# Where the second normalisation of the next token block is issued in the MLP loop of a state-space and MLP layer

## The chip, the cores and the metric

The kernel runs on one core of one Trainium2 chip. The metric is the device time of one execution in microseconds (us). The matrix multiplies run on TensorE (PE in the profile; its weight loads are listed as PEld), the rest on VectorE (DVE), ScalarE (ACT) and GpSimd (POOL). SyncE (SP) starts most of the transfers. Each engine works through its own list of instructions in the order in which the program put them there.

## What is computed

The layer has two halves on 2048 tokens of 640 channels. The first normalises the tokens, runs a short and a long convolution over them and adds the gated result to the input. The second normalises again and applies an MLP with a squared relu. Cut to what matters:

```python
def _layernorm(x, axis=-1, eps=1e-5):
    m = jnp.mean(x, axis=axis, keepdims=True)
    v = jnp.var(x, axis=axis, keepdims=True)
    return (x - m) / jnp.sqrt(v + eps)

def _B_ref(x, w1, b1, w2, b2):          # w1: 640 x 1728, w2: 1728 x 640
    h = jnp.einsum("bsd,df->bsf", x, w1) + b1
    r = jnp.where(h > 0, h, 0)
    h = r * r
    return jnp.einsum("bsf,fd->bsd", h, w2) + b2

h = _layernorm(x) * (1 + ca) + sa
x = x + ga * _A_ref(h, k, v, shift_k, ssm_k, ssm_D)
h = _layernorm(x) * (1 + cb) + sb
x = x + gb * _B_ref(h, w1, b1, w2, b2)
```

The vectors sa, ca, ga, sb, cb and gb come from one small conditioning vector. The change lies in the last two lines, in the second normalisation.

## The kernel before, in words

The first 290 us or so are the convolution half, and the change doesn't touch them. The MLP half goes through the tokens in `NC` = 8 blocks of 256 (n = 0 to 7), and in each block through the 1728 hidden channels in `NF` = 14 groups (f = 0 to 13; thirteen of 128 and a last one of 64). The loop at the end of the kernel (from line 1206) has one step for each pair (n, f), and the work of one pair is spread over several steps. A step i puts these pieces down, in this order:

- `mlp_back` of the pair three steps earlier (`MLAG` = 3): the second matrix multiply, twelve matmuls at L790, which reads the hidden values from a ring of buffers (`hring`) and adds into four accumulators in PSUM.
- `mlp_split` of the pair one step earlier: ScalarE copies the squared values to a high half (L146, in the helper `copy`), VectorE subtracts to get the low half (L157, in the helper `sub`). Both halves go to `hring`.
- `mlp_front` of this pair: the first matrix multiply, fifteen matmuls at L720 (ten at L711 for the last group), into one of two PSUM buffers.
- `mlp_front_end` of this pair: relu with bias on ScalarE (L752), then the square on GpSimd (L151).
- what prepares the next block, n + 1, spread over the steps of block n.

The preparation of block n + 1 goes like this for n of 1 and more. At f = 3 the block's 256 tokens are loaded (`load_x1`). At f = 5 VectorE makes means and variances, and at f = 6 ScalarE takes the root and VectorE makes the two vectors `rs2` and `nm2`. `prep_hat(n + 1, i)` (L670) then normalises 128 tokens by 640 channels in one ScalarE instruction at L672, i = 0 for the first 128 tokens of the block and i = 1 for the second. The result goes to `ML["xh"][i]`, which is a part of the tile `mtmp`; the relu's output lies in other parts of that tile. From f = 8 to f = 12 `prep_xt(n + 1, b)` handles one of five groups of 128 channels in each step: two transposes on TensorE (L685), one from each `ML["xh"][i]`, a scale and shift on VectorE (L687), a copy to the high half on ScalarE and a subtraction to the low half on GpSimd. While n is 0 the same work for block 1 has other places, since the weights are still being loaded then.

After the block's last group `mlp_end` and `mlp_out` use the same two `ML["xh"]` buffers for the gated output; this ends in the step f = 2 of the next block.

All instructions of an engine are tied into the order in which they were put down (`keep_order`, L118), so the place of a call in the loop decides what stands ahead of it and behind it on its engine. The two calls before the change, from L1236:

```python
                if f - (5 if n == 0 else 7) in (0, 1):
                    prep_hat(n + 1, f - (5 if n == 0 else 7))
                if f >= 8 and f - 8 < NB:
                    (prep_xt if n else prep_xt2)(n + 1, f - 8)
```

Of the kernel before, what the change touches and what calls it, by code (L numbers as in the profile page):

```python
# [92 lines left out]
def ssm_mlp_kernel(  # L93
# [549 lines left out]
    def stats2(n):  # L643
        for l in (2 * n, 2 * n + 1):
            if n:
                dve_stats(mv2[:, l], X1t[n][:, l - 2 * n])
            else:
                dve.bn_aggr(mv2[:, l], st2[:, l])

    def stats2_root(n):  # L650
        s = slice(2 * n, 2 * n + 2)
        act.activation(rs2[:, s], mv2[:, s, 1], AF.Sqrt, bias=eps_t)

    def stats2_end(n):
        s = slice(2 * n, 2 * n + 2)
        dve.reciprocal(rs2[:, s], rs2[:, s])
        dve.scalar_tensor_tensor(
            nm2[:, s], mv2[:, s, 0], -1.0, rs2[:, s], op0=ALU.mult, op1=ALU.mult
        )

    def load_x1(n):
        if n >= 2:
            X1t[n] = x1_tile(n)
            sp_dma(
                X1t[n], x1_d[n * CH : (n + 1) * CH, :].rearrange("(l p) d -> p l d", p=P)
            )
# [3 lines left out]
    def prep_hat(n, i):  # L670
        l = 2 * n + i
        act.activation(  # L672
            ML["xh"][i], X1t[n][:, i], AF.Identity, scale=rs2[:, l : l + 1], bias=nm2[:, l : l + 1]
        )
# [5 lines left out]
    def prep_xt1(n, b):  # L680
        if b == 0:
            XT[n] = sb.tile([P, 2, NB, CH], F32R, tag=f"XP{(n + 1) % 2}", name=f"xt_{n}")
        t = ps.tile([P, 2, P], F32, tag="Y", name=f"xtp_{n}_{b}", bufs=2)
        for i in range(2):
            pe.transpose(t[:, i], ML["xh"][i][:, b * P : (b + 1) * P], ident)  # L685
        f = ML["xf"][b % 2]
        dve.tensor_scalar(  # L687
            f,
            t.rearrange("p i s -> p (i s)"),
            cbs[:, 1, b : b + 1],  # L690
            cbs[:, 0, b : b + 1],
            op0=ALU.mult,
            op1=ALU.add,
        )
# [10 lines left out]
    def mlp_front(n, f, b):  # L705
        m = P if f < NF - 1 else 64
        if b == 0:
            hps[n, f] = ps.tile([P, CH], F32, tag="T", name=f"h_{n}_{f}", bufs=2)
        if m < P:
            for x in range(2):  # L710
                pe.matmul(  # L711
                    hps[n, f],
                    WI[1, f][:, b],
                    XT[n][:, x, b],
                    start=(b == 0 and x == 0),
                    stop=(b == NB - 1 and x == 1),
                )
            return
        for i, (a, x) in enumerate(((0, 0), (0, 1), (1, 0))):
            pe.matmul(  # L720
                hps[n, f][:m],
                WI[1, f][:, a, b],
                XT[n][:, x, b],
                start=(b == 0 and i == 0),
                stop=(b == NB - 1 and i == 2),
            )
# [15 lines left out]
    def mlp_front_end(n, f):  # L742
        m = P if f < NF - 1 else 64
        r = ML["r"][(n * NF + f) % 3]
        h = hps.pop((n, f))
        if m < P:

            act.activation(r[:m], h[m:], AF.Identity, bias=b1t[:m, f : f + 1])
            add(dve, r[:m], h[:m], r[:m])
            act.activation(r[:m], r[:m], AF.Relu)  # L750
        else:
            act.activation(r[:m], h[:m], AF.Relu, bias=b1t[:m, f : f + 1])  # L752
        mul(pool, r[:m], r[:m], r[:m])


    def mlp_split(n, f):
        m = P if f < NF - 1 else 64
        k = n * NF + f
        r = ML["r"][k % 3]
        if k == 2:  # L760
            hr = sb.tile([P, 4, 2, CH], F32R, tag="UP0", name="hring")
            ML["h"] += [hr[:, i] for i in range(4)]
        h = ML["h"][k % 6]
        if m == P:
            copy(act, h[:, 0], r)
            sub(dve, h[:, 1], r, h[:, 0])
        else:
            copy(act, h[:m, 0], r[:m])
            sub(dve, h[m:, 0], r[:m], h[:m, 0])
        hs[n, f] = h  # L770

    def mlp_back(n, f):
        if f == 0:
            accs[n] = [
                ps.tile([P, 320], F32, tag="X", name=f"acc_{n}_{i}", bufs=4) for i in range(4)
            ]
        acc = accs[n]
        h, w = hs[n, f], WI[2, f]
        if f < NF - 1:
            terms = ((0, 0), (0, 1), (1, 0))  # L780
        else:
            terms = ((0, 0), (0, 1))
        order = [(s, ti, i) for s in range(2) for ti in range(len(terms)) for i in range(2)]
        if f == NF - 1:
            order.sort(key=lambda o: (o[0], o[2]))
        for s, ti, i in order:
            if True:
                a, y = terms[ti]
                if True:
                    pe.matmul(  # L790
                        acc[2 * s + i],
                        h[:, a, s * P : (s + 1) * P],
                        w[:, y, i * 320 : (i + 1) * 320],
                        start=(f == 0 and ti == 0),
                        stop=(f == NF - 1 and ti == len(terms) - 1),
                    )

    def mlp_end(n):
        for s in range(1 if n == NC - 1 else 2):
            mlp_gate(n, s, 0)  # L800
            mlp_gate(n, s, 1)
# [5 lines left out]
    def mlp_out(n):  # L807
        for s in range(2):
            t = ML["xh"][s]
            l = 2 * n + s  # L810
            if n < NC - 1:
                add(dve if s else pool, X1t[n][:, s], t, X1t[n][:, s])
                sp_dma(out[l * P : (l + 1) * P, :], X1t[n][:, s])
                continue
            for i in range(2):
                o = slice(i * 320, (i + 1) * 320)
                if s:
                    mlp_gate(n, s, i)
                add(dve if s else pool, X1t[n][:, s, o], t[:, o], X1t[n][:, s, o])
                (act.dma_start if i else sp_dma)(out[l * P : (l + 1) * P, o], X1t[n][:, s, o])  # L820
# [363 lines left out]
    def residual(n, i, eng):  # L1184
        add(eng, X1t[n][:, i], X1t[n][:, i], row1b[0])

    def beside(f):
        n = min(len(stage), 6 + 2 * f)
        if f == 2:
            stats2(1)  # L1190
        while wn[0] < n:
            w_high()
        while wn[1] < n:
            w_low(dve)
        while len(stage) - wn[1] < 4 and items:
            load_item()
        if f < 3:
            finish_add(NB - 1, f + 1)
        if f == 0:
            finish_near(NB - 1, 1)  # L1200
        if f == 2:
            stats2_root(1)
        if f == 3:
            stats2_end(1)
# [3 lines left out]
    for i in range(len(seq) + MLAG):  # L1208
        if i >= MLAG:
            n, f = seq[i - MLAG]  # L1210
            mlp_back(n, f)
            if f == NF - 1:
                mlp_end(n)
        if 0 < i <= last + 1:
            mlp_split(*seq[i - 1])
        if i >= MLAG and f == NF - 1:
            mlp_out(n)
        if i <= last:
            n, f = seq[i]
            if i >= 2:  # L1220
                for b in range(NB):
                    mlp_front(n, f, b)
            mlp_front_end(n, f)
            if n == 0:
                if f >= 8 and f - 8 < NB:
                    prep_xt1(n + 1, f - 8)
                beside(f)
            if n + 1 < NC:
                if f == 3:
                    load_x1(n + 1)  # L1230
                if n and f == 5:
                    stats2(n + 1)
                if n and f == 6:
                    stats2_root(n + 1)
                    stats2_end(n + 1)
                if f - (5 if n == 0 else 7) in (0, 1):  # L1236
                    prep_hat(n + 1, f - (5 if n == 0 else 7))
                if f >= 8 and f - 8 < NB:
                    (prep_xt if n else prep_xt2)(n + 1, f - 8)
            if f >= 11 and f < 13:  # L1240
                residual(n, f - 11, pool)
# [25 lines left out]
```

## Time and profile before

| | us |
|---|---|
| median of 3 runs | 703.28 |
| lowest and highest run | 702.06, 704.84 |
| the profiled execution, its time | 705.5 |
| its span, first to last instruction | 703.7 |
| L720 matmuls, 1290 | 167.5 busy |
| L790 matmuls, 960 | 156.6 busy |
| L672 normalisations, 14 | 0.912 each (median) |
| mean clock granted to TensorE | 0.992 of full speed |

Times in the profile count from the first instruction of the profiled execution. A group in the profile is named by line, engine and operation, then what it writes and reads ("mtmp<-x,nm,rs" writes mtmp from x, nm and rs). "Idle before" is the time in which the engine stood still just ahead of an instruction, with the one that released it. The chain of work is followed back from the last instruction, at each step to what released it or to the instruction before it on its engine. Matmuls are pipelined and overlap in the records, so the starts of the pieces of the chain tell more than their lengths, and the end of a matmul is modelled.

### The profile page before, as it was taken

What the parts mean: (1) busy time and instruction counts of PE and PEld (TensorE: products, weight loads), DVE (VectorE), ACT (ScalarE), POOL (GpSimd) and SP (SyncE); (2) the same over time, 40 slices, a digit from 0 to 9 for tenths busy, and PEclk for the clock granted to TensorE, in tenths of its full rate; (3) what the DMA queues carried; (4) which work ended last, traced back from release to release, by engine and by line L of the source; (5) the groups of instructions that cost most, each with busy time, mean ns of one, the idle gap of its engine ahead of it and who ended that gap; (6) DMA issues with size and microseconds to landing.
All of it is one profiled execution on the core that took longest, in us unless ns stands there. A gap on an engine that the chain in (4) does not pass through costs nothing.

```text
span 703.7 us, 21084 instructions
## 1 busy us (share of the span) xinstructions
PE 662.0 (94%) x9164; PEld 634.2 (90%) x9164; DVE 334.6 (48%) x601; ACT 329.6 (47%) x688; POOL 311.2 (44%) x390
## 2 busy tenths in 40 slices
PE   6699799999999989999999999999999999999997
PEld 5688788888898888899999999999999999999996
DVE  5257666657684886587522323323332322422313
ACT  4436556877967966566233333233233233233221
POOL 1053155459869859433514414315215215224213
PEclk9999999999999999999999999999999999999999
DMA  9887889798672645274010100200200200200001
GB/s 232 248 240 235 238 238 250 232 231 219 181 186 82 158 126 172 69 227 142 39 38 1 42 35 1 74 3 1 75 1 1 76 1 1 76 1 1 38 1 38
DMA packets 110960, 74.76 MB, mean 106 GB/s; under 512 B 48658, under 2 KB 96146, under 8 KB 110868
## 3 DMA queue, kind: packets, MB, share of 16 engines
q1 hardware_dynamic: 108912, 72.87, 36.5%
q8 instruction: 72, 1.18, 0.7%
q10 hardware_dynamic: 1892, 0.54, 0.3%
q14 instruction: 20, 0.16, 0.1%
q0 software_dynamic: 64, 0.01, 0.0%
HBM read 58.98 MB, written 14.42 MB: 104 GB/s over the span
## 4 chain that ended last, share of the span: by engine, by line
PE 83%; ACT 6%; DVE 5%; issue 3%; DMA 2%; POOL 1%; SPq 0%; DVEq 0%; ACTq 0%; POOLq 0%
PE acc L790 27%; PE h L720 25%; PE pa L383 5%; PE x L398 5%; PE qp L464 5%; PE y L541 5%; PE h L398 3%; PE t L530 2%; PE h L711 1%; PE xtp L685 1%; PE kt L239 1%; DVE wx L151 1%; ACT a L146 1%; PE vt L276 1%; PE gr L928 1%
## 5 line engine op out<-in xcount | busy, mean ns | idle before, releaser
L151 POOL TENSOR_TENSOR mtmp<-mtmp 128x256 f32<-128x256 f32 x112 | 71.4, 638 | 244.4 <-ACT mtmp L752 236.5
L720 PE MATMUL h<-xt,w_S 128*128 128x256 f32 x1290 | 167.5, 281 | 1.1 <-DVE w_S L157 1.1
L720 PEld LDWEIGHTS h<-xt,w_S 128*128 128x128 f32 x1290 | 161.7, 190 | 1.3 <-DVE w_S L157 1.3
L790 PE MATMUL acc<-w_S,hring 128*128 128x320 f32 x960 | 156.6, 311 | 0.2 <-DVE hring L157 0.2
L157 DVE TENSOR_TENSOR hring<-mtmp,hring 128x256 fp32r<-128x256 f32 x112 | 66.4, 593 | 162.6 <-ACT hring L146 162.6
L790 PEld LDWEIGHTS acc<-w_S,hring 128*128 128x128 f32 x960 | 142.0, 188 | 0.7 <-DVE hring L157 0.7
L752 ACT ACTIVATE mtmp<-h,b1t 128x256 f32<-128x256 f32 x104 | 49.4, 475 | 180.1 <-PE h L720 177.0
L146 ACT ACTIVATE hring<-mtmp 128x256 fp32r<-128x256 f32 x112 | 46.6, 416 | 48.5 <-POOL mtmp L151 47.5
L383 PE MATMUL pa<-wx,p 64*64 64x64 f32 x2560 | 49.7, 228 | 10.9 <-issue 5.3
L383 PEld LDWEIGHTS pa<-wx,p 64*64 64x64 f32 x2560 | 44.1, 141 | 17.2 <-issue 11.3
L146 ACT ACTIVATE a<-pa 128x512 f32<-128x512 f32 x80 | 43.6, 611 | 22.9 <-PE pa L383 22.8
L151 DVE TENSOR_TENSOR wx<-x,wx 128x512 f32<-128x512 f32 x64 | 41.0, 684 | 19.4 <-PE x L398 8.9
L541 PE MATMUL y<-wx,wx 128*64 128x64 f32 x1280 | 45.4, 226 | 4.5 <-ACT wx L146 2.7
L541 PEld LDWEIGHTS y<-wx,wx 128*64 128x64 f32 x1280 | 40.7, 139 | 9.5 <-issue 4.2
L687 DVE TENSOR_SCALAR we<-xtp,cbs 128x256 f32<-128x256 f32 x35 | 19.0, 544 | 61.1 <-PE xtp L685 61.1
L398 PE MATMUL x<-a,gb 128*64 128x128 f32 x640 | 43.8, 281 | 3.0 <-DVE wx L151 1.8
L398 PEld LDWEIGHTS x<-a,gb 128*64 128x64 f32 x640 | 37.7, 141 | 4.4 <-PE h L398 2.4
L261 DVE SCALAR_TENSOR_TENSOR KV<-kt,tap,KV 128x511 f32<-128x511 f32 (+2 forms) x48 | 35.9, 747 | 8.1 <-ACT ktail L146 6.3
L154 POOL TENSOR_TENSOR wm<-wm,wm 128x640 f32<-128x640 f32 x20 | 32.9, 1647 | 10.3 <-ACT wm L341 10.0
L146 ACT ACTIVATE q<-qp 128x512 f32<-128x512 f32 (+1 forms) x40 | 21.3, 585 | 33.1 <-PE qp L464 33.1
L157 POOL TENSOR_TENSOR we<-wx 128x256 f32<-128x256 f32 x20 | 15.8, 789 | 47.0 <-DVE wx L151 46.1
L398 PE MATMUL h<-a,gb 128*64 128x128 f32 x512 | 34.4, 275 | 0.6 <-ACT wx L146 0.6
(142 smaller groups left out, 1032.7 us busy)
## 6 DMA issues: line engine op xcount, KB each, us to landing
wm<-in_w_mod_dram SPq DMA_DIRECT2D x25, 320.0 KB, 4.2
KV<-in_A_k_dram SPq DMA_DIRECT2D x20, 256.0 KB, 4.6
KV<-in_A_v_dram SPq DMA_DIRECT2D x20, 256.0 KB, 4.5
p<-in_A_ssm_k_dram SPq DMA_DIRECT2D x20, 256.0 KB, 4.9
p<-kv_d SPq DMA_DIRECT2D x20, 256.0 KB, 4.8
xp<-in_A_q_dram SPq DMA_DIRECT2D x20, 256.0 KB, 4.5
q<-in_A_q_dram SPq DMA_DIRECT2D x15, 320.0 KB, 5.0
out_dram<-x SPq DMA_DIRECT2D x14, 320.0 KB, 2.2
```

The costliest lines, as they stand in the source:

```text
L146: act.activation(o, i, AF.Copy)
L151: eng.tensor_mul(o, a, b)
L154: eng.tensor_add(o, a, b)
L157: eng.tensor_sub(o, a, b)
L261: dve.scalar_tensor_tensor(o, tk[:, : 512 - t], tap[:, b, t : t + 1], o, op0=ALU.mult, op1=ALU.add)
L383: pe.matmul(t[e][64 * r : 64 * r + 64, g].rearrange("p m d -> p (m d)"), pt[b][l, i, 8 * q + g, :], cw[l, r], start=True, stop=True,)
L398: pe.matmul(t[64 * a : 64 * a + 64, s + r], gb[:, g, r, a], AX[b][i][:, 2 * g + a], start=True, stop=True,)
L464: pe.matmul(t[a][:, u], gi[l, 4 * j + u, r], w[r][l, u % 2], start=(r == 0), stop=(r == 1),)
L541: pe.matmul(y[64 * h : 64 * h + 64, 4 * (g % 2) + i].rearrange("p c l d -> p (c l d)"), tss[g][:, i, 64 * r : 64 * r + 64], ca[:, r, h], s ...
L720: pe.matmul(hps[n, f][:m], WI[1, f][:, a, b], XT[n][:, x, b], start=(b == 0 and i == 0), stop=(b == NB - 1 and i == 2),)
L752: act.activation(r[:m], h[:m], AF.Relu, bias=b1t[:m, f : f + 1])
L790: pe.matmul(acc[2 * s + i], h[:, a, s * P : (s + 1) * P], w[:, y, i * 320 : (i + 1) * 320], start=(f == 0 and ti == 0), stop=(f == NF - 1 ...
```

## The change

The second normalisation of the next block, `prep_hat(n + 1, 1)`, is put down at f = 7, right behind the first, instead of at f = 8. This holds for n from 1 to 6. For n = 0 both calls stay where they were (f = 5 and f = 6). The transposes stay at f = 8 to f = 12.

```diff
                 if n and f == 6:
                     stats2_root(n + 1)
                     stats2_end(n + 1)
-                if f - (5 if n == 0 else 7) in (0, 1):
-                    prep_hat(n + 1, f - (5 if n == 0 else 7))
+                if n == 0 and f in (5, 6):
+                    prep_hat(1, f - 5)
+                if n and f == 7:
+                    prep_hat(n + 1, 0)
+                    prep_hat(n + 1, 1)
                 if f >= 8 and f - 8 < NB:
                     (prep_xt if n else prep_xt2)(n + 1, f - 8)
```

## The prediction

> **What bounds the kernel now.** I read the page first: the busy shares, and the chain of work that ended last.
>
> ```profile
> PE 662.0 (94%) x9164; PEld 634.2 (90%) x9164; DVE 334.6 (48%) x601; ACT 329.6 (47%) x688; POOL 311.2 (44%) x390
> ...
> PE 83%; ACT 6%; DVE 5%; issue 3%; DMA 2%; POOL 1%; SPq 0%; DVEq 0%; ACTq 0%; POOLq 0%
> PE acc L790 27%; PE h L720 25%; PE pa L383 5%; PE x L398 5%; PE qp L464 5%; PE y L541 5%; PE h L398 3%; PE t L530 2%; PE h L711 1%; PE xtp L685 1%; PE kt L239 1%; DVE wx L151 1%; ACT a L146 1%; PE vt L276 1%; PE gr L928 1%
> ```
>
> TensorE sets the time, and the two matmul lines of the MLP (L790 is the second, L720 the first) make up half of the chain. The other engines are busy less than half of the span. So an edit on ScalarE matters only where TensorE waits for ScalarE. Whether it does at the normalisation (L672, `prep_hat`) I asked of that line's own view.
>
> ```profile
> L672 ACT ACTIVATE mtmp<-x,nm,rs x14: 908/912/917, 312.6 to 626.0; 128x640 f32<-128x640 f32 x14
> L672 ACTq EVENT_SEMAPHORE  x6: 17/17/17, 366.7 to 622.1; - x6
> ...
> who waited for it (us, times):
>   PEld xtp L685: 9.3, 6
>   PE xtp L685: 7.9, 6
> ```
>
> Fourteen normalisations run through L672: two for each of seven token blocks. TensorE waited for six of them, at the transposes (L685). The 7.9 us is the matmul row's idle time, the 9.3 us the weight load row's. They are the same six waits seen from two rows and are not added. Six is also the number of blocks for which the diff moves something: those prepared while n is 1 to 6. The block prepared at n = 0 keeps its places.
>
> Next the chain in order of time, around the third of the six (columns: start us, length us, what), with the first and the last of the six below it and the end of the matmuls.
>
> ```profile
> 465.22 1.76 PE acc L790 x12
> 466.98 1.77 PE h L720 x15
> 468.75 1.76 PE acc L790 x12
> 470.50 1.78 PE h L720 x15
> 472.29 0.02 issue
> ...
> 472.37 0.47 ACT mtmp L752
> 472.85 0.82 ACT mtmp L672
> 473.66 0.04 issue
> 473.71 0.33 PE xtp L685
> 474.03 1.76 PE acc L790 x12
> 475.80 1.78 PE h L720 x15
> 477.58 0.22 PE xtp L685 x2
> 477.80 1.76 PE acc L790 x12
> ...
> 366.55 1.76 PE acc L790 x12
> ...
> 371.84 1.77 PE acc L790 x12
> ...
> 375.62 1.76 PE acc L790 x12
> ...
> 622.02 1.76 PE acc L790 x12
> ...
> 627.31 1.76 PE acc L790 x12
> ...
> 631.07 1.76 PE acc L790 x12
> ...
> 693.77 3.83 PE acc L790 x26
> ```
>
> A step of the loop is twelve L790 matmuls of three steps earlier, then fifteen L720 matmuls of this one. The run that starts at 466.98 belongs to f = 7, the run at 470.50 to f = 8. A plain step takes 468.75 - 465.22 = 3.53 us, and TensorE has no hole in it. In the f = 8 step the chain leaves TensorE: after the L720 run ends at 472.29 it goes through the relu of f = 8 (L752), then the second normalisation (L672), and comes back for one transpose at 473.71. ScalarE can't start the relu before the L720 run is done, the normalisation is queued behind the relu, and the transposes need it at the very moment at which the relu may start. That is a wait built into the order of the instructions. The steps after it have transposes too, but they cost 0.22 us and no wait.
>
> **The change, part by part.** Two calls of `prep_hat` are made at f = 7 instead of one at f = 7 and one at f = 8. It adds no instruction and no transfer, and touches no queue but ScalarE's. One ACTIVATE of 128x640 (median 912 ns) moves from behind the relu of f = 8 to a place ahead of the high-half copy of f = 7 and of that relu. The semaphore event of 17 ns stands once in each of the six blocks, and I count it at nothing.
>
> *What is removed.* The transposes' stall: 472.29 to 474.03 is 1.74 us, where an undisturbed pair of transposes takes 0.22, so 1.52 us. From L790 start to L790 start: the f = 8 step takes 474.03 - 468.75 = 5.28, the next one with its pair 477.80 - 474.03 = 3.77; the difference is 1.51. The first stall gives (371.84 - 366.55) - (375.62 - 371.84) = 5.29 - 3.78 = 1.51, the last (627.31 - 622.02) - (631.07 - 627.31) = 5.29 - 3.76 = 1.53. Six times 1.51 is 9.06 us. The idle of the matmul row alone (7.9) leaves out that a restarted transpose takes 0.33 us where two in stride take 0.22; that makes it the lower bound, and the weight loads' 9.3 the upper.
>
> *What is moved, and where it lands.* ScalarE's timeline at the same stall, with one line of VectorE's and one of TensorE's (start, length, instruction, idle time before it and its releaser).
>
> ```profile
> 468.84 0.48 ACT L752 ACTIVATE mtmp<-h,b1t 128x256 f32<-128x256 f32 x1 [1.97 <-PE h L720]
> 469.22 0.91 ACT L672 ACTIVATE mtmp<-x,nm,rs 128x640 f32<-128x640 f32 x1
> 470.04 0.42 ACT L146 ACTIVATE hring<-mtmp 128x256 fp32r<-128x256 f32 x1
> 472.37 0.47 ACT L752 ACTIVATE mtmp<-h,b1t 128x256 f32<-128x256 f32 x1 [1.91 <-PE h L720]
> 472.75 0.91 ACT L672 ACTIVATE mtmp<-x,nm,rs 128x640 f32<-128x640 f32 x1
> ...
> 470.49 0.43 DVE L157 TENSOR_TENSOR hring<-mtmp,hring 128x256 fp32r<-128x256 f32 x1 [3.16 <-ACT hring L146]
> ...
> 477.68 0.48 ACT L752 ACTIVATE mtmp<-h,b1t 128x256 f32<-128x256 f32 x1 [2.30 <-PE h L720]
> ...
> 477.42 0.38 PE L685 MATMUL xtp<-ident,mtmp 128*128 128x128 f32 x2
> ```
>
> The first normalisation starts at 469.22 and the next instruction at 470.04, so one in a row takes 0.82 us of the engine. The second one needs nothing the first didn't: the same two columns of roots and means, the other half of the same loaded tile. Its target, the second half of `ML["xh"]`, was last read at f = 2. So it would run 470.04 to 470.95. The transposes, due at 472.29, find it done 1.3 us before.
>
> What stands behind it on ScalarE gets later by 0.82 us. The copy of f = 7 moves from 470.04 to 470.86 and ends at 471.28; ScalarE was idle for 1.91 us before the relu at 472.37, and 1.09 of that is left, so the relu and all that follows it start as they did. VectorE's low half (470.49) is released by that copy: it moves to about 471.31 and ends near 471.74. That engine had nothing else to do there. The consumer is the L790 run of f = 7 in the step f = 10, at 477.80, which moves up by the removed 1.51 to 476.29: still 4.5 us later. So this edit costs nothing, and what covers it is the L720 run of f = 8. Without that cover it would cost the 0.82 us.
>
> [...]
>
> *The sum.* The profiled execution has a span of 703.7 us and took 705.5; its new span would be 703.7 - 9.06 = 694.6 and its time 696.4. It was 2.2 us above the median of the runs (703.28, from 702.06 to 704.84). I put the saving against the median: 703.28 - 9.06 = 694.2 us.
>
> **The rivals.**
>
> 1. *The transposes really hang on the relu.* The wait is put down to L672, but it is a count of ScalarE's finished instructions. If the wait left after the move were one for the relu of f = 8, which ends at 472.85, then L790 would start 0.37 us later (as 474.03 stands to 473.66), at 473.22. That saves 0.81 us in a block, 4.9 in all: 698.4. Against it: the pair at 477.42 runs with no idle time before it while the relu of its own step starts only at 477.68.
>
> 2. *The delay on ScalarE comes to the path.* The 0.82 us comes back through the copy, the low half and L790: 1.51 - 0.82 = 0.69 a block, 4.1 in all: 699.1. It needs over 4.5 us of further delay to reach L790, or over 1.09 us to reach the relu. The durations of L672 (908 to 917 ns in all fourteen) show no such stretching.
>
> 3. *Nothing changes: 703.3.* The second normalisation would have to wait at f = 7 for something that arrives only at f = 8. Its inputs are those of the first, which ran at 469.22 with no idle time before it.
>
> 4. *Slower: TensorE is granted a lower clock once it has no pauses.* The stretch from 366.55 to the end of the matmuls at 697.60 is 331.0 us, and 322.0 after the change. The gain is eaten from a clock of 322.0 / 331.0 = 0.973 downward. The lowest that a window of this trace has is 0.95: 322.0 / 0.95 = 339.0, hence 694.2 + 17.0 = 711.2. The view of busy time by windows bears on it (window, length, busy time by engine, granted clock, DMA share, GB/s).
>
> ```profile
> 0.00:100.00 100.00, 82.11 (x1942) 74.13 (x1943) 54.77 (x107) 47.27 (x91) 27.90 (x65) 0.95 0.87 236
> 448.08:465.22 17.14, 17.14 (x134) 17.14 (x133) 7.29 (x16) 4.47 (x10) 4.84 (x6) 1.00 0.21 77
> 474.03:477.80 3.77, 3.77 (x32) 3.77 (x31) 1.30 (x2) 0.84 (x3) 0.74 (x1) 1.00 0.00 0
> ```
>
> The low value stands where TensorE was least busy, while 17 us without any hole run at 1.00. So does the step right behind the stall, which also means that there is no second gain from a clock that the stalls had lowered.
>
> **How the numbers follow.** The forecast has a chance of 0.90: cause and count are in the rows, and the six stalls are alike within 0.02 us. Rivals 1 and 2 have 0.03 each, 3 has 0.02, 4 has 0.02. The time is the forecast's, 694.2. For the range I take the bounds of the saving (9.3 and 7.9) with the lowest and the highest of the runs: 702.06 - 9.3 = 692.8 and 704.84 - 7.9 = 696.9, rounded outward to 692.5 and 697.0. The rivals lie outside and hold 0.10. A measurement of this kernel can tell about 0.5% (3.5 us) from no change. The forecast and rivals 1 and 2 are faster by more than that (9.1, 4.9 and 4.1 us): 0.96. Rival 3 is the same: 0.02. Rival 4 is slower: 0.02.
>
> **What would show it.** In the profile after, L672 should have no waiter on TensorE, where it had six. The chain around each place should read L790, L720, a pair of transposes of 0.22, L790, with 3.75 to 3.8 us from L790 to L790. ScalarE should show two L672 in a row 0.82 us apart, then the copy, then about 1.1 us of idle time until the relu. Two stalls in a row should be about 49.6 us apart in place of 51.1, which is (627.31 - 371.84) / 5. I'd be wrong in the cause if the transposes are still idle with another releaser, wrong in the cover if the relu's idle time at f = 8 is gone or L790 waits for `hring`, and wrong on the clock if windows inside the MLP show less than 1.00.

## The result, and the profile after

The changed kernel takes 693.53 us in the median of 4 runs (692.88 to 696.69), the kernel before 704.06 (702.06 to 705.56, 4 runs). The ratio is 0.9866 with a 95% interval of 0.9835 to 0.9897. The median moved by 10.5 us where 9.1 were forecast, and the interval reaches from 7.3 to 11.6 us. The span of the profiled execution went from 703.7 to 691.8 us, that is by 11.9.

In the view of the normalisation's line, the list of those who waited for it is now empty. Before, it held the six waits of TensorE.

```profile
L672 ACT ACTIVATE mtmp<-x,nm,rs x14: 908/912/915, 310.6 to 612.9; 128x640 f32<-128x640 f32 x14
L672 ACTq EVENT_SEMAPHORE  x6: 17/17/17, 364.0 to 611.7; - x6
its engine sat idle before it (us, times) until:
who waited for it (us, times):
```

A transpose that waited for the relu instead would not stand in this list. So here are also all waits of TensorE's matmuls between 300 and 700 us in the changed kernel (line, releaser, line of the releaser, us in all, times, longest); the one that is left stands in block 0.

```profile
PE h L720 <- DVE w_S L157: 1.1, 1, 1.1
```

The chain of waits of the changed kernel (start, length, what), at the start of the loop, around two of the six places, and at the end of the matmuls:

```profile
301.93 1.81 PE h L720 x13
...
417.15 1.76 PE acc L790 x12
...
462.96 1.76 PE acc L790 x12
464.72 1.77 PE h L720 x15
466.49 0.22 PE xtp L685 x2
466.71 1.76 PE acc L790 x12
468.47 1.78 PE h L720 x15
470.25 0.22 PE xtp L685 x2
470.47 1.76 PE acc L790 x12
...
681.80 3.83 PE acc L790 x26
```

The chain no longer leaves TensorE: the first pair of transposes takes 0.22 us like the second. The step with the first pair takes 466.71 - 462.96 = 3.75 us, where it took 5.28. That is 1.53 to 1.54 us a block (1.51 was forecast, from the next step's 3.77 us). Two blocks stand 466.71 - 417.15 = 49.56 us apart, in place of 51.1.

The same place on ScalarE, from the timeline (start, length, instruction, idle time before it and its releaser):

```profile
463.06 0.48 ACT L752 ACTIVATE mtmp<-h,b1t 128x256 f32<-128x256 f32 x1 [1.97 <-PE h L720]
463.43 1.73 ACT L672 ACTIVATE mtmp<-x,nm,rs 128x640 f32<-128x640 f32 x2
465.06 0.40 ACT L146 ACTIVATE hring<-mtmp 128x256 fp32r<-128x256 f32 x1
466.59 0.47 ACT L752 ACTIVATE mtmp<-h,b1t 128x256 f32<-128x256 f32 x1 [1.12 <-PE h L720]
```

The two normalisations take 1.63 us from the start of the first to the start of the copy. The relu of f = 8 still waits for TensorE, now 1.12 us instead of 1.91.

To see where the 11.9 us of the span come from, I cut it at the L720 run of 13 matmuls, which opens the undisturbed part of the loop, and at the end of the matmuls. In the kernel before, the chain has that run here:

```profile
304.62 1.81 PE h L720 x13
```

| | before | after | difference |
|---|---|---|---|
| up to the L720 run of 13 | 304.62 | 301.93 | 2.69 |
| from there to the end of the last matmul (start of the run of 26, plus 3.83) | 392.98 | 383.70 | 9.28 |
| the rest | 6.1 | 6.2 | -0.1 |

9.28 us are where the change is, six times 1.55. The other 2.7 lie ahead of it, in code that is the same in both. The run of the unedited changed kernel, further down, bears on them.

### The profile page after: what moved, and what is told of

Same layout as the page of the kernel before. It is cut to its first block, busy times and chain, and to the rows that moved or that the text cites. A ratio compares the mean times of both kernels' runs of the same rounds, so it can differ in the third digit from the quotient of the medians.

```text
span 691.8 us, 21084 instructions
## 1 busy us (share of the span) xinstructions
PE 659.1 (95%) x9164; PEld 632.5 (91%) x9164; DVE 335.0 (48%) x601; ACT 329.8 (48%) x688; POOL 310.7 (45%) x390
## 4 chain that ended last, share of the span: by engine, by line
PE 82%; DVE 5%; ACT 5%; DMA 4%; issue 3%; POOL 1%; DVEq 0%; POOLq 0%; ACTq 0%; SPq 0%
PE acc L790 27%; PE h L720 26%; PE qp L464 5%; PE x L398 5%; PE pa L383 5%; PE y L541 3%; PE h L398 3%; PE t L530 2%; PE h L711 1%; DMA wm<-in_w_mod_dram 1%; DMA p<-kv_d 1%; PE xtp L685 1%; ACT a L146 1%; DVE wx L151 1%; DVE KV L261 1%
## 5 line engine op out<-in xcount | busy, mean ns | idle before, releaser
L720 PE MATMUL h<-xt,w_S 128*128 128x256 f32 x1290 | 167.5, 281 | 1.1 <-DVE w_S L157 1.1
L720 PEld LDWEIGHTS h<-xt,w_S 128*128 128x128 f32 x1290 | 161.7, 190 | 1.3 <-DVE w_S L157 1.3
L790 PE MATMUL acc<-w_S,hring 128*128 128x320 f32 x960 | 156.6, 311 | 0.2 <-DVE hring L157 0.2
L790 PEld LDWEIGHTS acc<-w_S,hring 128*128 128x128 f32 x960 | 141.7, 188 | 0.8 <-DVE hring L157 0.7
L383 PE MATMUL pa<-wx,p 64*64 64x64 f32 x2560 | 51.5, 230 | 11.3 <-issue 5.1
L398 PE MATMUL x<-a,gb 128*64 128x128 f32 x640 | 42.2, 274 | 3.0 <-DVE wx L151 1.7
L398 PEld LDWEIGHTS x<-a,gb 128*64 128x64 f32 x640 | 36.2, 137 | 4.6 <-PE h L398 2.4
```

What stands on the lines that cost most here:

```text
L383: pe.matmul(t[e][64 * r : 64 * r + 64, g].rearrange("p m d -> p (m d)"), pt[b][l, i, 8 * q + g, :], cw[l, r], start=True, stop=True,)
L398: pe.matmul(t[64 * a : 64 * a + 64, s + r], gb[:, g, r, a], AX[b][i][:, 2 * g + a], start=True, stop=True,)
L720: pe.matmul(hps[n, f][:m], WI[1, f][:, a, b], XT[n][:, x, b], start=(b == 0 and i == 0), stop=(b == NB - 1 and i == 2),)
L790: pe.matmul(acc[2 * s + i], h[:, a, s * P : (s + 1) * P], w[:, y, i * 320 : (i + 1) * 320], start=(f == 0 and ti == 0), stop=(f == NF - 1 ...
```

## The experiments

"The stretch" below is the middle row of that table. It is read from the chain of each kernel's own profile. The three kernels with more normalisations were executed once each.

| kernel | L720 run of 13 starts | end of matmuls | stretch |
|---|---|---|---|
| before | 304.62 | 697.60 | 392.98 |
| changed | 301.93 | 685.63 | 383.70 |
| second normalisation ahead of the relu | 306.08 | 689.78 | 383.70 |
| changed for half of the blocks | 303.80 | 692.13 | 388.33 |
| both behind the relu | 304.82 | 703.78 | 398.96 |
| changed, five more | 304.08 | 687.73 | 383.65 |
| changed, eight more | 307.78 | 704.05 | 396.27 |
| changed, ten more | 301.50 | 714.36 | 412.86 |
| changed, again | 304.86 | 688.57 | 383.71 |

**Is it the relu, or the step?** The second normalisation goes back to f = 8, but ahead of that step's relu.

```diff
                 if n and f == 7:
                     prep_hat(n + 1, 0)
-                    prep_hat(n + 1, 1)
...
+            if n and n + 1 < NC and f == 8:
+                prep_hat(n + 1, 1)
             mlp_front_end(n, f)
```

> The second normalisation goes back to the step f = 8, but is put ahead of that step's relu instead of behind it. Theory (the stall comes only from standing behind a relu that waits for TensorE): ScalarE runs it in the idle time before the relu, it ends about 0.9 us before the transposes are due, and the whole gain stays: 383.7 us from the L720 run of 13 matmuls at the start of the loop to the end of the matmuls, as with the change (393.0 before), and no waiter of L672 on TensorE. Rival (the normalisation has to be a whole step earlier, whatever it stands behind): the stalls come back, 393.0 us. Second rival (the change also made the convolution half shorter, 301.9 us until that L720 run in place of 304.6): near 301.9 here too; if that is scatter it falls anywhere between about 300 and 306.

Measured: 383.70 us, to the hundredth what the change gives, and no waiter. The time is 0.989 of before (0.986 to 0.993). ScalarE's timeline of this kernel:

```profile
468.41 0.42 ACT L146 ACTIVATE hring<-mtmp 128x256 fp32r<-128x256 f32 x1
468.73 0.91 ACT L672 ACTIVATE mtmp<-x,nm,rs 128x640 f32<-128x640 f32 x1
470.74 0.47 ACT L752 ACTIVATE mtmp<-h,b1t 128x256 f32<-128x256 f32 x1 [1.10 <-PE h L720]
```

The normalisation runs in the idle time before the relu. So between these two places the step doesn't matter; only the relu ahead of it did, which waits for TensorE. The first rival of this experiment falls. So does the second: the L720 run of 13 starts at 306.08 here, 4 us later than in the changed kernel's profile.

**Does each block pay for itself?**

```diff
                 if n and f == 7:
                     prep_hat(n + 1, 0)
-                    prep_hat(n + 1, 1)
+                    if n < 4:
+                        prep_hat(n + 1, 1)
+                if n >= 4 and f == 8:
+                    prep_hat(n + 1, 1)
```

> The change is made for n = 1 to 3 alone; n = 4 to 6 keep the old order. Theory: each block is worth 1.54 us by itself, so the stretch from the L720 run of 13 to the end of the matmuls is 393.0 - 3 * 1.545 = 388.4 us, the time about 4.6 us under before (ratio 0.993), and L672 has three waiters on TensorE. Rival (the gain is one effect of the whole loop, such as a better phase or clock, not a sum over blocks): 383.7 or 393.0.

Measured: 388.33 us, half of the way (4.65 of 9.28). The time is 0.996 of before (0.993 to 0.999). Those who waited for L672 in this kernel:

```profile
who waited for it (us, times):
  PEld xtp L685: 4.7, 3
  PE xtp L685: 4.0, 3
```

Half of the waits, and half of their time. The gain is a sum over blocks.

**What if both stand behind the relu?**

```diff
-                if n and f == 7:
+                if n and f == 8:
                     prep_hat(n + 1, 0)
                     prep_hat(n + 1, 1)
```

> Both normalisations are put down at f = 8, behind the relu, and none at f = 7. Theory: the stall grows by one normalisation in a row, 0.82 us, in each of the six blocks: 1.51 + 0.82 = 2.33 us a stall, 393.0 + 6 * 0.82 = 397.9 us for the stretch, some 5 us over before (ratio 1.007). Rival (the wait hangs on the relu, or on something else that ends at the same time): 393.0 us.

Measured: 398.96 us, and a time of 1.010 of before (1.007 to 1.014). The direction is the theory's, the rival's 393.0 us falls, and the size is 1.1 us over the theory. The chain of this kernel around one ordinary stall and around another that behaves differently:

```profile
470.44 1.76 PE acc L790 x12
...
476.48 1.76 PE acc L790 x12
478.24 1.78 PE h L720 x15
...
528.31 2.58 PE acc L790 x12
530.89 2.48 PE h L720 x15
533.37 0.22 PE xtp L685 x2
533.59 1.76 PE acc L790 x12
```

The ordinary step takes 476.48 - 470.44 = 6.04 us, 0.76 more than before; I had put 0.82. Six times that is 4.6. Behind the fourth stall the same twelve and fifteen matmuls take 2.58 and 2.48 us instead of 1.76 and 1.78. This adds 533.59 - 528.31 = 5.28 in place of 3.76, so 1.5 us. Together that is 6.1, and 5.98 were measured. The view by windows of the same kernel shows why (window, length, busy time of the five rows of engines, granted clock, DMA share, GB/s):

```profile
525.20:527.70 2.50, 0.92 (x7) 0.53 (x5) 0.00 (x0) 1.87 (x3) 0.61 (x1) 1.00 0.00 0
...
529.50:531.30 1.80, 1.80 (x9) 1.80 (x8) 0.75 (x1) 0.15 (x1) 0.65 (x1) 0.50 0.00 0
```

The clock granted to TensorE is half for 3.4 us behind this hole (0.97, 0.50, 0.50, 0.50 and 0.82 in the five windows of 1 us from 528 to 533), and behind none of the other five.

**How much does ScalarE's delay cost?** The changed kernel with five or eight more normalisations behind the two, written to a buffer that nothing reads. They are extra work; nothing is left out. All that follows on ScalarE is later by them.

```diff
                 if n and f == 7:
                     prep_hat(n + 1, 0)
                     prep_hat(n + 1, 1)
+                    for _ in range(5):
+                        pad_hat(n + 1)
...
+    def pad_hat(n):
+        t = sb.tile([P, D], F32, tag="STG", name="pad", bufs=4)
+        act.activation(t, X1t[n][:, 1], AF.Identity, scale=rs2[:, 2 * n + 1 : 2 * n + 2], bias=nm2[:, 2 * n + 1 : 2 * n + 2])
```

> The changed kernel with five more normalisations of 128x640 behind the two at f = 7, n = 1 to 6, written to a buffer that nothing reads. They delay the high-half copy of f = 7 and all behind it on ScalarE by 5 * 0.82 = 4.1 us a block. Theory (4.5 us of cover at the second multiply): VectorE's low half ends at about the time when L790 of f = 7 wants it, so at most 0.2 us a block comes to TensorE: 383.7 to 385 us from the L720 run of 13 to the end of the matmuls. Rival (the cover is the 1.1 us of ScalarE's idle time ahead of the relu, and what exceeds it reaches TensorE): 4.1 - 1.1 = 3.0 us a block, 401.7 us.

> The same with eight more: 6.56 us of delay a block. Theory: L790 of f = 7 waits for hring until the low half is done, 6.56 - 4.3 = about 2.3 us a block, 383.7 + 13.6 = 397.3 us for the stretch, with L790 waiting for VectorE's L157 six times. Rival (cover of 1.1 us): 5.5 us a block, 416.5 us.

Measured: 383.65 us with five more, so 4.1 us of delay in each block cost nothing. The relu of f = 8 then starts right behind the copy, with no idle time before it and 2.9 us after its L720 run ended at 468.63:

```profile
471.57 0.45 ACT L756 ACTIVATE mtmp<-h,b1t 128x256 f32<-128x256 f32 x1
```

So the idle time ahead of the relu isn't what has to cover the delay. With eight more it is 396.27, where 397.3 was the theory's and 416.5 the rival's. The timeline with eight more, at the place where it hurts (the added function moves the line numbers: L794 is L790 of before):

```profile
481.26 0.40 ACT L146 ACTIVATE hring<-mtmp 128x256 fp32r<-128x256 f32 x1
...
481.70 0.43 DVE L157 TENSOR_TENSOR hring<-mtmp,hring 128x256 fp32r<-128x256 f32 x1 [10.72 <-ACT hring L146]
...
481.72 2.77 PE L794 MATMUL acc<-w_S,hring 128*128 128x320 f32 x12 [1.82 <-ACT hring L146]
482.04 0.54 DVE L691 TENSOR_SCALAR we<-xtp,cbs 128x256 f32<-128x256 f32 x1
```

L794 is released by ScalarE's copy and not by VectorE's subtraction, which only starts then. The expectation named VectorE, and that was wrong: the first four matmuls of a run read the high half alone. The timeline shows VectorE's order as well: L691's transposes are done at 479.90 (the pair starts at 479.52 and takes 0.38), and it comes at 482.04, behind the subtraction that was put down ahead of it. From the chain with eight more, the restarts of L794 behind the holes:

```profile
378.77 2.02 PE acc L794 x12
...
430.10 2.02 PE acc L794 x12
...
534.58 2.03 PE acc L794 x12
```

Blocks are 430.10 - 378.77 = 51.33 us apart, 1.77 more than the 49.56 of the changed kernel. The eight normalisations take 6.50 us in this chain, and TensorE stood idle for 1.53 us ahead of an ordinary restart, so about 5.0 us were covered; the restarted run is 0.26 us longer than an undisturbed one. Six times 1.77 is 10.6 of the 12.6 us by which the stretch grew, where the theory had 13.6. Most of the rest is one fall of the clock that the theory didn't have, so it is partly luck that its 397.3 lies near the measured 396.27. One block, from 481.72 to 534.58, takes 52.86: there the L794 run behind the hole took 2.77 us where the others took 2.02. The windows of this kernel give the clock granted during that run and the one after it:

```profile
481.70:484.48 2.78, 2.76 (x13) 2.77 (x14) 1.99 (x4) 1.41 (x4) 1.99 (x3) 0.68 0.00 0
484.48:487.06 2.58, 2.58 (x19) 2.58 (x17) 0.85 (x2) 0.72 (x2) 0.84 (x2) 0.68 0.00 0
```

In this kernel TensorE was idle for 9.5 us in the six holes. The one of 1.82 us ahead of this drop is the longest, the other five have 1.5 on the mean.

**Does the clock fall because of the holes?** Ten more, for larger holes still.

> The changed kernel with ten more normalisations at f = 7 that nothing reads: TensorE is held up for about 1.79 + 2 * 0.82 = 3.43 us in each of six blocks. With eight more, the clock granted fell behind one of six holes (idle 1.8 us in the matmul row), and behind none of the 1.3 us holes of before. Theory (the clock falls when a hole covers enough of a free-running stretch of some 3 us): holes of 3.4 us lower it in most or all of the six blocks, about 1.5 us each: 383.7 + 6 * 3.43 + 4 to 6 times 1.5 = 410 to 413 us from the L720 run of 13 to the end of the matmuls. Rival (the single drop was chance that has nothing to do with the hole): 404.3 us.

Measured: 412.86 us. TensorE was idle for 18.9 us in six holes, 3.15 each. The chain of this kernel behind three of the six, and its windows around the second and the fourth:

```profile
429.65 2.43 PE acc L794 x12
432.07 2.91 PE h L724 x15
...
538.60 2.03 PE acc L794 x12
540.63 1.80 PE h L724 x15
...
591.56 3.53 PE acc L794 x12
```

```profile
431.00:433.00 2.00, 2.00 (x11) 2.00 (x10) 1.20 (x2) 1.09 (x4) 1.49 (x2) 0.52 0.00 0
...
538.60:540.60 2.00, 2.00 (x14) 2.00 (x15) 1.21 (x3) 1.39 (x4) 1.23 (x2) 1.00 0.00 0
```

Five of the six runs of L794 and L724 behind the holes are stretched, the fourth is not. The theory holds in its number of blocks and in its sum. Its free-running stretch of some 3 us was an assumption that no run had shown by then; the falls of this run lie on cells of 3.41 us (last section). Why the fourth is spared, with a hole as long as the others, stands in the last section.

**Is the convolution half part of it?** The changed kernel once more.

> The changed kernel once more, unedited. Theory: 383.7 us for the stretch to within 0.1, and a convolution half that differs from the 301.9 us of the first profile by more than that, since it differs between executions. Rival (the change shortened the convolution half): 301.9 us again.

Measured: a stretch of 383.71 us, and 304.86 us up to it where the first profile had 301.93. The time is 0.987 of before (0.983 to 0.991). One and the same kernel differs by 2.9 us ahead of the loop. So the 2.7 us of the first table need no cause in the change, and all nine rows of the table of stretches lie between 301.5 and 307.8. A part of the scatter may be the clock: ahead of 290 us it falls to half for 3.4 us three times in the profile of before (at 29.7, 36.5 and 77.4 us), once in that of the changed kernel and twice in this one. But the number of falls doesn't put all nine rows in order (with ten more it is two, and that row starts earliest), so the rest stays open.

**Another wait of the same kind.** In the changed kernel one L720 run still waits 1.06 us, at f = 3 of block 0, for the low half of a weight that stands on VectorE behind the statistics of block 1. First the statistics were put behind the weights of the same step:

```diff
     def beside(f):
         n = min(len(stage), 6 + 2 * f)
-        if f == 2:
-            stats2(1)
         while wn[0] < n:
             w_high()
         while wn[1] < n:
             w_low(dve)
+        if f == 2:
+            stats2(1)
```

(with the root and the vectors of block 1 together at f = 3).

> The changed kernel, and in block 0 the statistics of block 1 (two pairs of bn_stats on VectorE, 2.0 us in all) are put behind the low halves of the weights of the step f = 2 instead of ahead of them, their root on ScalarE a step later. With the change a L720 run waits 1.06 us for such a low half. Theory (same cause, a wait behind work that could come later): that wait goes and 1.1 to 1.5 us come off the stretch, 382.2 to 382.6 in place of 383.7. Rival (VectorE is the bound there, and the next low half is late instead): 383.7.

The chain of this kernel doesn't pass the L720 run of 13, so I compare from the L734 run of 29 ahead of it: 293.98 to 690.53 is 396.55 us, and 289.11 to 685.63 in the changed kernel is 396.52. Nothing is gained; the rival holds. TensorE's timeline of this kernel:

```profile
305.88 1.82 PE L720 MATMUL h<-xt,w_S 128*128 128x256 f32 x13 [0.16 <-DVE w_S L157]
...
308.94 1.44 PE L790 MATMUL acc<-w_S,hring 128*128 128x320 f32 x8 [0.65 <-DVE hring L157]
```

The wait for the weight is gone but for 0.16 us, and the next thing on VectorE is late in its place: the low half for `hring`, now behind the statistics. So the statistics have to leave that step altogether, one half to f = 3 and one to f = 4:

```diff
-        if f == 2:
-            stats2(1)
...
+        if f in (3, 4):
+            dve_stats(mv2[:, f - 1], X1t[1][:, f - 3])
...
-        if f == 2:
-            stats2_root(1)
-        if f == 3:
-            stats2_end(1)
+        if f == 4:
+            stats2_root(1)
+            stats2_end(1)
```

> The changed kernel, and in block 0 the statistics of block 1 are put down half in the step f = 3 and half in f = 4, each behind the low halves of that step's weights, with root and vectors at f = 4, ahead of the first normalisation at f = 5. With the statistics at the end of f = 2 nothing was gained, since VectorE then came late with the next hring half (0.65 us of waiting in place of 1.06). Theory (VectorE has room again from f = 3 on): the wait of 1.06 us goes and no new one comes; from the L734 run of 29 to the end of the matmuls 395.5 us in place of 396.5. Rival (the low halves themselves, of which two took 1.9 us beside GpSimd's work, are the bound): 396.5.

Measured: 289.49 to 685.03, so 395.54 us, 0.98 less. TensorE's one wait left between 300 and 700 us is this:

```profile
PE h L720 <- DVE w_S L157: 0.2, 1, 0.2
```

The time is 694.1 us in the median of 4 (0.982 of before, 0.976 to 0.989). In the trace this kernel is 1.0 us better than the changed one; the intervals of the two times overlap, so the times alone can't tell them apart.

## Why the prediction was right

*The wait.* Its step holds: six waits, each made of the relu and the normalisation behind it, and nothing else. Taking the normalisation out from behind the relu in another way gives the same 383.70 us, and doing it for three blocks gives half. Rival 1 (a wait for the relu itself) falls with the chain, where the first pair takes 0.22 us and the step 3.75, and with the list of TensorE's waits, where no transpose is left. Rival 3 (an input that comes late) falls with the empty list of waiters.

*The size.* 9.06 us were forecast and 9.28 measured in the stretch. The term was short by 0.03 to 0.04 us a block: I took the next step's 3.77 us as the length of an undisturbed step with transposes, but the first one of a block takes 3.75, and with its stall it had taken 5.28 to 5.29.

*The moved instruction.* The forecast was that ScalarE keeps 1.09 us of idle time before the relu; 1.12 is there. The prediction also said what covers the delay, the L720 run of f = 8, and that without it the change would cost the 0.82 us. That was wrong: with five more that idle time is gone, and the stretch is 383.65 us. What covers the delay is the distance to the next use on TensorE. It was put at 4.5 us, from VectorE's low half to L790. What L790 waits for first is the high half from ScalarE, and about 5.0 us are covered; the prediction's own rows give the same for it (476.29 - 471.28 = 5.01). The second rival (the 0.82 us returns) needed a delay of more than the 4.1 us that cost nothing, several times the 0.82 us that the change makes.

*The clock.* The fourth rival expected a lower clock from a denser TensorE. No such thing: from 301.93 to 685.63 us the clock granted in the changed kernel is 1.00, and its stretch repeats to 0.01 us. Inside the loop it fell only behind holes. The 0.95 that the prediction took as the lowest is the mean of a window of 100 us; from 30 to 32 us the same trace has 0.50, so the rival's price was no upper bound.

*The time.* 694.2 us was forecast and 693.53 measured. The span was forecast at 694.6 and is 691.8; the difference is the 2.7 us ahead of the loop, by which single executions of one kernel differ, plus the 0.2 of the size. That the median came within 0.7 us of the forecast is partly luck, since four later runs of the same kernel had a median of 695.78.

## What to carry to other kernels

When an engine with slack holds up the one without, look at what the late instruction is queued behind: here a relu that could not start before the bottleneck had finished its step (1.91 us of idle time ahead of it), so that everything behind it was late by construction. Moving it ahead of that one instruction was all that was needed. How much can be put there is said by the distance to the next use on the bottleneck engine (5.0 us here), and not by the idle time ahead of the relu (1.1 us). On an engine that was full in that step, as VectorE with the weights (no idle time from 299.20 to 312 us with the statistics put later), moving within the step only handed the wait on (1.06 us became 0.16 and 0.65); the work had to go to a step with room.

## What the runs showed of the hardware that was not expected

Holes in TensorE's work cost more than their length in some places of these runs. Behind the six holes of 1.3 us of the kernel before, the clock stayed at 1.00. With both normalisations behind the relu (1.85 us of idle time in a hole, a lone transpose in its middle) it fell behind one of six, down to 0.50 in a window of 1.8 us. With eight more (1.5 to 1.8 us) it fell behind one of six, and with ten more (3.15 us) behind five of six. Each fall cost 1.5 us or more.

Which holes do it can be read from the traces. With ten more, the clock falls at 373.04, 431.06, 485.68, 591.48 and 646.10 us (worked out from the granted clock in windows of 1 us). The later four are 17, 33, 64 and 80 times 3.413 us behind the first. Each fall lasts 3.4 us, the first twice that. Two falls ahead of the loop, at 28.30 and 86.32, fit too (17 times 3.413 apart, and the first of the loop 101 times behind 28.30). In the profile of before the falls stand at 29.65, 36.48 and 77.44, the later two 2 and 14 times 3.413 behind the first, and the first of them ends at 33.07, 3.41 us on. So in both executions the falls lie on a grid of cells of 3.41 us, with ten more from 28.30 to 646.10 us. Two cells of the kernel with ten more with a hole in them, each with the cell behind it (columns as above, TensorE's matmuls first):

```profile
482.26:485.67 3.41, 1.54 (x10) 1.54 (x11) 0.88 (x2) 2.82 (x7) 0.76 (x2) 1.00 0.00 0
485.67:489.08 3.41, 3.41 (x18) 3.41 (x17) 1.96 (x3) 1.17 (x4) 2.07 (x3) 0.50 0.00 0
...
536.87:540.29 3.42, 1.69 (x11) 1.69 (x12) 0.92 (x3) 2.83 (x7) 0.92 (x2) 1.00 0.00 0
540.29:543.70 3.41, 3.41 (x29) 3.41 (x28) 2.38 (x4) 1.69 (x5) 2.55 (x4) 1.00 0.00 0
```

In the first cell TensorE is idle for 3.41 - 1.54 = 1.87 us, and the next cell runs at half. The fourth hole of this kernel is as long as the others, but an edge of the grid parts it into 1.42 and 1.73 us, and the clock stays. In the loops of the three kernels with falls, the cells ahead of the seven falls had 1.82 to 3.16 us of idle time, and no cell without a fall behind it more than 1.73. In these loops the border thus lay between 1.73 and 1.82 us in one cell, about half of it, and whether a hole of 1.8 to 3.2 us cost anything depended on where it stood in the grid. What held the first fall with ten more for a second cell, with about 1.1 us of idle time in the cell ahead (from 373.04 to the restart at 374.11), the runs don't show. This was read from the traces afterwards; no run was made to test it, and ahead of the loop one fall (both behind the relu, at 242.2 us) has only 0.76 us of idle time in the cell before it.
